# The first x block in five transfers instead of two, and its casts in a new order

## The chip, the cores and the metric

The kernel runs on one core of one Trainium2 chip. The metric is the device time of one execution in microseconds (us); less is better. Times given as "span" are those of one profiled execution, from its first to its last instruction.

## The reference

Two layers follow each other. The first is a causal convolution with weights of its own at every position: `weight_gen` (8 x 4096 x 8 heads x 7 taps) goes through a softmax over the 7 taps, and each position of `x` (8 x 4096 x 192) becomes, head by head (24 columns each), the weighted sum of itself and the six positions before it. The second is a feed-forward layer with squared ReLU.

```python
w = weight_gen - np.max(weight_gen, axis=-1, keepdims=True)
w = np.exp(w)
w = w / (np.sum(w, axis=-1, keepdims=True) + 1e-09)
x_pad = np.concatenate([np.zeros((B, pad, D)), x], axis=1)      # pad = 6
x_unf = x_pad[:, idx, :].reshape(B, S, K, H, group)             # seven shifted views
x = np.einsum('bshk,bskhg->bshg', w, x_unf).reshape(B * S, D)   # 32768 x 192
h = np.maximum(x @ w_in, 0.0)                                   # 192 x 2048
out = h * h @ w_out                                             # 2048 x 192
```

## The kernel before

All matmuls are in fp16 with f32 sums. The 32768 positions are cut into sub-blocks of 512. The first two blocks hold one sub-block each, all later blocks two. Within a sub-block the convolution works on five tiles of 128 rows of x, each 104 rows after the one before (`NT = 5`, `STEP = 104`); a tile covers 104 outputs (the last 96) and the rows ahead that their taps need.

For each tile three things must exist before TensorE can convolve it: the softmax weights of its 128 rows (`wr`), a banded matrix made of them on VectorE (`bd`, `st_band`, L406), and the x tile in fp16 (`xt`). The convolution's matmuls (L466 in the first two blocks) write `yp` in PSUM; two casts make it `y` (ScalarE L476, VectorE L477). `y` goes through w_in (L566, later L581) to `h`, ScalarE applies ReLU (L595), VectorE squares (L599), and TensorE multiplies by w_out (L630).

The order of all work is written out by hand: engines run their instructions in program order, and the transfers of one queue are issued in program order too. Two queues matter here, that of SyncE (SP in the profile) and that of GpSimd (POOL). A transfer of f32 data that POOL issues may cast to fp16 on the way; SP's transfers do not cast, so what SP loads is cast by an engine afterwards.

The start, which is where the change lies, goes as follows.

- SP issues the loads of the first 1024 positions' weights (`s0.load`, three transfers, `wg`, L219), then the first sub-block's x in f32 (`x_load_f32(0)`, `x_st`): tile 0 alone (L317) and tiles 1 to 4 in one transfer (L327), both through `block_load`. Then the first half of w_in in f32 (`load_w_in(w_st, 0, nc.sync)`, three transfers, L133 and L135).
- POOL waits at a small copy (`gate`, L716) until the softmax's reciprocals exist, and then issues the second sub-block's x, the second half of w_in and the next weights. A second such copy (L746) waits for `w_st`; behind it POOL issues w_out (L183) and more.
- TensorE spins on zeros (L697) until the softmax of the first rows is scaled (`v_first`, L266). It then brings the rows of weights to the partitions where the tiles want them by matmuls with a selection matrix (`select_rows`, L383, eight matmuls a tile), first the five tiles of sub-block 0, then the five of sub-block 1, and then convolves.
- ScalarE takes the exponentials (L244), casts x tile 0 (`x_cast`, L342), copies the selected rows of tiles 0 and 1 out of PSUM (`copy_rows`, L391), casts x tiles 1 and 2 in one instruction, copies the rows of tiles 2 to 4, casts x tiles 3 and 4, copies the rows of sub-block 1 in one instruction, casts one part of `w_st` to `w_i` (`cast_w_in`, L740), and casts `y`. VectorE makes the five bands, casts the other half of `y`, and then the other part of `w_st` (L740 as well).

In the code before, the part of this order that the change touches reads:

```python
x_cast(0, nc.scalar.copy, 0, 1)
o0, o1, ring = (ps_o, "o0"), (ps_o, "o1"), (ps_h, "h")
select_rows(0, s0, ROW_ORDER, (o1, ring, ring, ring, o0))
copy_rows(0, ROW_ORDER[:2])
x_cast(0, nc.scalar.copy, 1, 3)
copy_rows(0, ROW_ORDER[2:])
x_cast(0, nc.scalar.copy, 3, NT)
```

After the start, blocks follow each other with the w_in units of one block, the w_out matmuls of the block before and the convolution of the block after woven into each other by written plans.

Of the kernel before, what the change touches and what calls it, by code (L numbers as in the profile page):

```python
# [9 lines left out]
def kernel(  # L10
# [26 lines left out]
    nc = tc.nc  # L37
# [3 lines left out]
    B, S, D = x.shape  # L41
# [9 lines left out]
    P = 128  # L51
    TB = 512
    NBB = S // TB
# [12 lines left out]
    NT = 5  # L66
# [4 lines left out]
    ROW_ORDER = (0, 1, 2, 3, 4)  # L71
# [57 lines left out]
    x_st = {}  # L129
# [167 lines left out]
    def rows(ap2d, t0, width):  # L297

        return bass.AP(
            tensor=ap2d.tensor, offset=ap2d.offset + t0 * width,  # L300
            ap=[[width, P], [STEP * width, NT], [1, width]],
        )

    def ends(b):
        rs = PARTS.get(b, (R,))
        return [P * sum(rs[: i + 1]) for i in range(len(rs))]

    def tile_start(j, i):

        t1 = (j % NBB + 1) * TB  # L310
        return TB - P if i == NT - 1 and t1 in ends(j // NBB) else starts[i]

    def block_load(j, dst, src, width, eng):
        t0 = (j % NBB) * TB
        first, last = int(t0 == 0), NT
        if first:
            eng.dma_start(out=dst[:, 0], in_=src[0:P, :])  # L317
        a = t0 + tile_start(j, NT - 1)
        if a != t0 + starts[-1]:
            last = NT - 1  # L320
            eng.dma_start(out=dst[:, last], in_=src[a : a + P, :])
        ap = rows(src, t0 + starts[first], width)
        ap = bass.AP(
            tensor=ap.tensor, offset=ap.offset,
            ap=[ap.ap[0], [STEP * width, last - first], ap.ap[2]],
        )
        eng.dma_start(out=dst[:, first:last], in_=ap)  # L327
# [4 lines left out]

    def x_load_f32(j):
        x_st[j] = p_one.tile([P, (R + HALO) * HK], f32, name="x_st", tag="ex")
        block_load(
            j, x_st[j][:, 0 : NT * D].rearrange("p (t d) -> p t d", t=NT), x[j // NBB], D, nc.sync
        )

    def x_cast(j, copy, lo, hi):
        if j not in x_t:  # L340
            x_t[j] = p_x.tile([P, NT, D], f16, name="xt")
        copy(  # L342
            out=x_t[j][:, lo:hi].rearrange("p t d -> p (t d)"),
            in_=x_st[j][:, lo * D : hi * D],
        )
# [23 lines left out]
    def select_rows(j, s, tiles, places):  # L369

        if j not in wr_t:
            wr_t[j] = p_wr.tile([P, NT, HP, SL * 2], f16, name="wr")
        n = len(tiles) // len(places)
        for m, i in enumerate(tiles):
            if m % n == 0:
                pool, tag = places[m // n]
                prs = pool.tile([P, n, H * SL], f32, name="pr", tag=tag)
                pr_t[(j, i)] = prs
            pr = prs[:, m % n]
            a = max(j % NBB * TB + tile_start(j, i), 0) - s.t0  # L380
            for r in range(s.r):
                c = a + FIRST - 1 - r
                nc.tensor.matmul(  # L383
                    out=pr, lhsT=sel[:, c : c + P],
                    rhs=s.v[:, HALO + r].rearrange("p g c e -> p (g c e)"),
                    start=(r == 0), stop=(r == s.r - 1),
                )

    def copy_rows(j, tiles, n=1):
        for i in tiles[::n]:  # L390
            nc.scalar.copy(  # L391
                out=wr_t[j][:, i : i + n].rearrange("p t g c -> p t (g c)"),
                in_=pr_t.pop((j, i)),
            )
# [271 lines left out]
    with nc.allow_low_precision("fp16 matmul pipeline"), tc.manual_schedule():  # L666
# [39 lines left out]
        s0.load(nc.sync, s0_cuts)  # L706
        w_st = p_wg.tile([P, (R + HALO) * HK], f32, name="w_st", tag="wg")[:, 0 : NQ + NQ // 2]
        x_load_f32(0)
        row_select()
        load_w_in(w_st, 0, nc.sync)  # L710
# [10 lines left out]
        x_cast(0, nc.scalar.copy, 0, 1)  # L721
        o0, o1, ring = (ps_o, "o0"), (ps_o, "o1"), (ps_h, "h")
        select_rows(0, s0, ROW_ORDER, (o1, ring, ring, ring, o0))
        copy_rows(0, ROW_ORDER[:2])
        x_cast(0, nc.scalar.copy, 1, 3)
        copy_rows(0, ROW_ORDER[2:])
        x_cast(0, nc.scalar.copy, 3, NT)
        for i in ROW_ORDER:
            st_band(0, (i,))
        select_rows(1, s0, ROW_ORDER, (o1,))  # L730
# [76 lines left out]
        for j in range(len(plans), NBLK - 1):  # L807
            a = BLOCKS[j + 1][0]
# [102 lines left out]
        j = NBLK - 1  # L911
# [44 lines left out]
```

## Time and profile before

| What | Value |
|---|---|
| Time of the timed runs | 730.38 us, median of 3 (729.42 to 730.4) |
| Span of the profiled execution | 728.4 us, 1.98 us under that median |
| TensorE busy | 722.0 us, 99% of the span |
| VectorE, ScalarE, GpSimd busy | 625.8 us (86%), 612.0 us (84%), 98.5 us (14%) |
| First w_in matmul of block 0 | at 12.20 us |
| Granted TensorE clock | 1.000 |

The profile is one execution; its own time is the span, and what the timed runs have beyond it lies around the first and last instruction or in differences from execution to execution. Lines of the profile name an engine, the line of the kernel (L342 is line 342), what is written and read, and how long. "PE" is TensorE, "DVE" VectorE, "ACT" ScalarE, "SPq" the instructions of SyncE that issue transfers. An idle time in brackets ends with what released it. A busy TensorE includes times that are modelled, so 99% says that it always had something to do and not that it ran at its peak.

### The profile page before, as it was taken

The numbers are of one execution on the slowest core, as the hardware profiler recorded it, in microseconds if no ns is written. First come the engines' busy times: TensorE is split into PE (matmuls) and PEld (weight loads), VectorE is DVE, ScalarE is ACT, GpSimd is POOL, SyncE is SP. The second block draws the span as 40 slices with busy tenths as digits, with TensorE's granted clock in tenths as the row PEclk, the third lists the DMA queues.
The fourth block names the chain that finished last, engine by engine and source line by source line (L and its number), as shares of the span: only waits on it lengthen the run. The fifth ranks groups of instructions, "written<-read, shape, count | busy, mean of one in ns | idle before, by whom it ended". The sixth has DMA issues, their size and how long they took to land.

```text
span 728.4 us, 31046 instructions
## 1 busy us (share of the span) xinstructions
PE 722.0 (99%) x14078; PEld 530.1 (73%) x14078; DVE 625.8 (86%) x839; ACT 612.0 (84%) x731; POOL 98.5 (14%) x146
## 2 busy tenths in 40 slices
PE   8999999999999999999999999999999999999998
PEld 5668877777777777777777777777777777777777
DVE  7999997998898998888988888988888988778753
ACT  6998888888888888888888888888888888888883
POOL 7231223411001100011001010010000110001000
PEclk9999999999999999999999999999999999999999
DMA  9664465676245443356432554343544325444112
GB/s 193 128 113 106 82 125 89 128 142 138 78 71 133 99 84 68 75 116 125 83 62 58 135 104 88 66 74 110 114 78 87 57 53 117 67 87 77 30 46 67
DMA packets 126272, 68.30 MB, mean 94 GB/s; under 512 B 85353, under 2 KB 122556, under 8 KB 125628
## 3 DMA queue, kind: packets, MB, share of 16 engines
q0 software_dynamic: 46192, 19.43, 22.9%
q1 hardware_dynamic: 79804, 46.79, 22.5%
q8 instruction: 110, 1.80, 1.1%
q14 instruction: 22, 0.18, 0.1%
q10 hardware_dynamic: 144, 0.10, 0.0%
HBM read 50.18 MB, written 28.70 MB: 108 GB/s over the span
## 4 chain that ended last, share of the span: by engine, by line
PE 98%; DMA 1%; SPq 0%; ACT 0%; issue 0%; ACTq 0%
PE o L630 47%; PE h L581 44%; PE yp L502 4%; PE h L566 2%; PE yp L536 1%; DMA w_st<-in_moe_w_in_dram 1%; SPq L219 0%; PE yp L466 0%; ACT w_i L740 0%; SPq L135 0%; SPq L133 0%; ACT y L476 0%; SPq L327 0%; SPq L317 0%; ACT o_sb L644 0%
## 5 line engine op out<-in xcount | busy, mean ns | idle before, releaser
L595 ACT ACTIVATE t<-h 128x1024 f16<-128x1024 f32 x512 | 496.6, 1027 | 60.1 <-PE h L581 58.4
L630 PEld LDWEIGHTS <-g 64*128 64x128 f16 (+1 forms) x8032 | 344.3, 94 | 55.2 <-issue 2.3
L630 PE MATMUL o<-w_o,g 64*128 64x192 f16 (+1 forms) x8032 | 380.1, 243 | 0.1
L599 DVE TENSOR_TENSOR g<-t 128x2048 f16<-128x2048 f16 (+1 forms) x287 | 307.4, 1105 | 28.7 <-ACT t L595 28.3
L581 PE MATMUL h<-y,w_p 64*128 64x512 f16 x2400 | 291.7, 376 | 0.0
L581 PEld LDWEIGHTS <-w_p 64*128 64x128 f16 x2400 | 113.9, 94 | 94.8
L406 DVE TENSOR_TENSOR bd<-wr,mask 128x4160 f16<-128x4160 f16 (+4 forms) x90 | 149.5, 1685 | 1.2 <-ACT wr L391 1.2
L646 DVE TENSOR_TENSOR o_sb<-o,o_sb 128x384 f32<-128x384 f32 x123 | 68.4, 556 | 61.4 <-ACT o_sb L644 60.3
L327 POOL DMA_DIRECT2D xt<-in_x_dram x63 | 52.6, 838 | 415.4 <-PE yp L502 362.5
L644 ACT COPY o_sb<-o 128x384 f32<-128x384 f32 x129 | 61.6, 477 | 45.7 <-PE o L630 44.4
L581 PE MATMUL h<-y,w_i 64*128 64x512 f16 x576 | 70.5, 376 | 0.0
L581 PEld LDWEIGHTS <-w_i 64*128 64x128 f16 x576 | 30.5, 94 | 21.7 <-issue 1.2
L502 PEld LDWEIGHTS <-xt 128*32 128x32 f16 x2000 | 24.6, 95 | 10.6 <-issue 10.6
L266 DVE TENSOR_TENSOR v_big<-ex,rcp 128x112 f16<-128x112 f32 (+5 forms) x180 | 29.9, 237 | 2.1 <-DMA vd<-v_big 1.1
L512 DVE CAST y<-yp 128x1024 f16<-128x1024 f32 x25 | 30.4, 1218 | 0.0
L502 PE MATMUL yp<-bd,xt 128*32 128x104 f16 (+1 forms) x2000 | 28.4, 210 | 0.0
L244 ACT ACTIVATE ex<-wg 128x560 f32<-128x560 f32 (+5 forms) x40 | 26.3, 659 | 1.2 <-DMA wg<-in_weight_gen_dram 1.2
L251 DVE TENSOR_REDUCE ssum<-ex 128x80 f32<-128x560 f32 (+5 forms) x40 | 25.6, 639 | 1.3 <-ACT ex L244 1.3
L512 ACT CAST y<-yp 128x1024 f16<-128x1024 f32 x25 | 25.2, 1007 | 0.0
L258 DVE RECIPROCAL rcp<-ssum 128x64 f32<-128x64 f32 (+4 forms) x39 | 23.0, 589 | 1.4
L317 POOL DMA_DIRECT2D xt<-in_x_dram x7 | 3.9, 555 | 120.4 <-PE yp L502 109.4
L361 POOL DMA_DIRECT2D wr<-v_first x24 | 13.0, 559 | 24.0 <-DVE v_first L266 23.8
(42 smaller groups left out, 111.9 us busy)
## 6 DMA issues: line engine op xcount, KB each, us to landing
out_dram<-o_sb SPq DMA_DIRECT2D x63, 384.0 KB
xt<-in_x_dram POOLq DMA_DIRECT2D x42, 240.0 KB, 4.9
wg<-in_weight_gen_dram SPq DMA_DIRECT2D x4, 1064.0 KB
xt<-in_x_dram POOLq DMA_DIRECT2D x21, 192.0 KB, 5.0
wr<-vd SPq DMA_DIRECT2D x38, 80.0 KB
vd<-v_big SPq DMA_DIRECT2D x5, 512.0 KB
y<-y SPq DMA_DIRECT2D x100, 24.0 KB
wg<-in_weight_gen_dram SPq DMA_DIRECT2D x3, 616.0 KB
```

The source lines that it names most:

```text
L244: nc.scalar.activation(out=self.ex[:, lo:hi].rearrange("p r g k e -> p (r g) k e"), in_=self.wg[:, lo:hi].rearrange("p r (g e) k -> p (r g ...
L266: eng.tensor_tensor(out=bass.AP(tensor=v.tensor, offset=v.offset + lo * H * SL + lo % SL * 2 + g * SL * 2, ap=[list(v.ap[0]), [H * SL + 2, ...
L327: eng.dma_start(out=dst[:, first:last], in_=ap)
L406: nc.vector.tensor_tensor(out=bd_t[j][:, H * lo : H * (lo + len(tiles) * n)].rearrange("p (g m c) -> p g m c", g=shape[1], c=2 * SL), in0= ...
L502: nc.tensor.matmul(out=yp[p0 : p0 + 32, k - k0, a:b], lhsT=x_t[s][:, i, c0 : c0 + 32], rhs=bd[:, head // 2, e, 0 : b - a], start=True, sto ...
L512: copy(out=y[:, k0 : k0 + 2], in_=yp)
L581: nc.tensor.matmul(out=h[:, half], lhsT=w_in_chunk(w, u, slot, half), rhs=y_t[j][r0 : r0 + RT, k], start=(slot == 0), stop=(slot == NK - 1 ...
L595: nc.scalar.activation(out=t1[:, e], in_=h, func=ActF.Relu)
L599: nc.vector.tensor_tensor(out=g[:, a : e + 1], in0=t1[:, a : e + 1], in1=t1[:, a : e + 1], op=AluOp.mult)
L630: nc.tensor.matmul(out=oo[:, cc * Dm : (cc + 1) * Dm], lhsT=g[r0 : r0 + n, cc * P : (cc + 1) * P], rhs=w_o[r0 : r0 + n, fc, :], start=(fc ...
L644: nc.scalar.copy(out=o_sb, in_=o[0][:, c])
L646: nc.vector.tensor_tensor(out=o_sb, in0=o[1][:, c], in1=o_sb, op=AluOp.add)
```

## The change

The first sub-block's x is loaded in five transfers, one for each tile of 128 rows, all issued by SP one after the other at the place where the two stood. Each tile is cast by an instruction of its own. The casts of tiles 1 and 2 stand ahead of the row copies, the five row copies follow without a break, and the casts of tiles 3 and 4 come after them. What is loaded, cast and copied is the same; no other line differs.

```diff
     def x_load_f32(j):
         x_st[j] = p_one.tile([P, (R + HALO) * HK], f32, name="x_st", tag="ex")
-        block_load(
-            j, x_st[j][:, 0 : NT * D].rearrange("p (t d) -> p t d", t=NT), x[j // NBB], D, nc.sync
-        )
+        for i in range(NT):
+            a = max(j % NBB * TB + tile_start(j, i), 0)
+            nc.sync.dma_start(
+                out=x_st[j][:, i * D : (i + 1) * D], in_=x[j // NBB, a : a + P, :]
+            )
...
         select_rows(0, s0, ROW_ORDER, (o1, ring, ring, ring, o0))
-        copy_rows(0, ROW_ORDER[:2])
-        x_cast(0, nc.scalar.copy, 1, 3)
-        copy_rows(0, ROW_ORDER[2:])
-        x_cast(0, nc.scalar.copy, 3, NT)
+        x_cast(0, nc.scalar.copy, 1, 2)
+        x_cast(0, nc.scalar.copy, 2, 3)
+        copy_rows(0, ROW_ORDER)
+        x_cast(0, nc.scalar.copy, 3, 4)
+        x_cast(0, nc.scalar.copy, 4, NT)
         for i in ROW_ORDER:
             st_band(0, (i,))
```

## The prediction

> **What bounds the kernel now.** First the page: TensorE holds the span, and the chain that ended last is TensorE's but for a little DMA.
>
> ```profile
> PE 722.0 (99%) x14078; PEld 530.1 (73%) x14078; DVE 625.8 (86%) x839; ACT 612.0 (84%) x731; POOL 98.5 (14%) x146
> ...
> PE 98%; DMA 1%; SPq 0%; ACT 0%; issue 0%; ACTq 0%
> ```
>
> The change lies in the first 12 us, so the chain of waits in order of time says what that part costs (start us, us, what):
>
> ```profile
> 2.67 0.43 SPq L327
> ...
> 3.15 0.51 SPq L133
> ...
> 3.70 0.59 SPq L135
> ...
> 4.33 6.39 DMA w_st<-in_moe_w_in_dram
> ...
> 10.83 0.83 ACT w_i L740
> 11.66 0.49 ACT y L476
> ...
> 12.20 3.17 PE h L566 x16
> ```
>
> From 12.20 us on the chain is TensorE without a gap worth naming (the table of busy time by stage gives it 17.00 of 17.00 us from 13 to 30). So the change is worth what it does to the 12.20, one for one, and to nothing else. What sets 12.20 is not x: it is w_st, the first half of w_in, cast at 10.83, and then y, cast behind it on the same in-order ScalarE.
>
> ScalarE in order of time shows what x costs (start, busy, then in brackets the idle time before and who ended it):
>
> ```profile
> 4.57 0.34 ACT L342 CAST xt<-x_st 128x192 f16<-128x192 f32 x1
> 7.58 0.45 ACT L391 CAST wr<-pr 128x64 f16<-128x64 f32 x2 [2.68 <-PE pr L383]
> 8.81 0.51 ACT L342 CAST xt<-x_st 128x384 f16<-128x384 f32 x1 [0.78 <-DMA x_st<-in_x_dram]
> 9.23 0.43 ACT L391 CAST wr<-pr 128x64 f16<-128x64 f32 x3
> 9.54 0.53 ACT L342 CAST xt<-x_st 128x384 f16<-128x384 f32 x1
> 9.95 0.45 ACT L391 CAST wr<-pr 128x320 f16<-128x320 f32 x1
> 10.83 0.83 ACT L740 CAST w_i<-w_st 128x768 f16<-128x768 f32 x1 [0.43 <-DMA w_st<-in_moe_w_in_dram]
> ```
>
> The cast at 8.81 waits 0.78 us for the four-tile x transfer, and row copies 2 to 4 wait behind it. That reaches the bands on VectorE and the first convolution:
>
> ```profile
> 7.90 1.09 DVE L406 TENSOR_TENSOR bd<-wr,mask 128x832 f16<-128x832 f16 x2 [0.75 <-ACT wr L391]
> 9.47 1.60 DVE L406 TENSOR_TENSOR bd<-wr,mask 128x832 f16<-128x832 f16 x3 [0.47 <-ACT wr L391]
> 11.54 0.69 DVE L477 CAST y<-yp 128x512 f16<-128x512 f32 x1 [0.47 <-PE yp L466]
> ```
>
> Two paths thus end nearly together: the convolution at 11.54, w_st's cast at 11.66.
>
> Why the four tiles take 6.14 us (2.67 to 8.81) is in the trace's packet records: on most DMA engines their 768-byte packets run from 4.1 to 6.0, but one packet begun at 5.66 took 1854 ns. That engine moved its last 13 x packets from 7.51 to 7.91 and only then its share of w_st, to 10.23; the others were through with w_st by 8.95. In the DMA view for 8.95 to 10.3 the queue of SP has 17 packets left:
>
> ```profile
> q1 hardware_dynamic: 17, 0.03, 5.7%
> ```
>
> **The change part by part.**
>
> *The convolution path.* The three row copies no longer sit behind a cast that waits. The selections give a tile every 0.25 us (78 matmuls in 2.44 us, eight a tile), so the last copy ends near 8.8. The bands, 0.545 us each (1.09 for two), then run without the 0.47 us gap from 7.90 to 10.63 instead of to 11.07: 0.44 us won, and the convolution ends near 11.10. The casts of tiles 1 and 2 (0.34 each) fit in ScalarE's idle 2.68 us ahead of 7.58; those of tiles 3 and 4 (0.68) come after 8.8, and the next copy must wait anyway for the second tile's selections (done at 9.65). ScalarE's casts grow from 1.38 to 1.70 us, hidden by those two idle stretches; without them 0.32.
>
> *When the tiles land.* The trace has no x transfer alone but tile 0. The loads of this size or near it on SP were usable 2.08, 2.32 and 2.43 us after issue (wg at 0.81, 1.26, 1.72, used at 2.89, 3.58, 4.15), tile 0 within 2.37. With issues at 2.67, 3.14, 3.61 and 4.08 this gives 5.1, 5.6, 6.0 and 6.5. The far end is the four-tile row, 6.14 after issue: tile 2 at 9.28. I take the near end for tiles 1 and 2, as they are the same shape as tile 0, and count the far end as a rival.
>
> The Trainium skill, "DMA: Bandwidth & Descriptors", "Rules for kernel authors", speaks against the change: many small transfers are to be joined into a large one, and its section on the anatomy of one DMA gives about 2.0 us of fixed cost each. Paid one after the other, three more would be an estimate of 6 us. The three wg loads, usable 0.57 to 0.69 us apart, say that these costs overlap.
>
> *Three more issues on SP.* One costs 0.47 us (0.43 and 0.04 to the next), three 1.41. All three w_st issues are moved behind them: from 3.15, 3.70, 4.29 to 4.56, 5.11, 5.70. The next item on SP, a row move (L361), started at 7.18 on VectorE's release, so SP has the room (6.3 against 7.18). POOL's issues keep their place; its gate at L746 waits for w_st as well (10.18), and behind it stand the four w_out loads. In the built order SP's transfers take eight completion semaphores in turn, and with five x transfers they wrap earlier: each w_st issue now waits for one of the wg loads. These were used at 2.89, 3.58 and 4.15, the issues' turns are 4.56, 5.11, 5.70: nothing, by 1.5 us or more. Later SP transfers still wait for the one eight before them, as now.
>
> *What of the 1.41 reaches w_st's landing.* Its packets now begin at 5.56, 2.4 us after issue, since x is ahead of them in each engine; a transfer that finds its queue empty begins 1.33 to 1.40 after issue (x tile 0: 2.20 to 3.53). So moved to 4.56 they begin near 5.96, 0.4 later. The rest is 8 packets of 159 ns and 8 of 84 ns an engine, 1.94 us: done at 7.9, used (0.6 later, as with the last packet at 10.23 and the cast at 10.83) at 8.5. ScalarE gets to that cast at 10.3 at the earliest, so the 1.41 is covered by 1.8 us of slack on an undisturbed engine. On an engine that stops on x as before, w_st queues behind it and lands when it does now, cost nothing. If the cover is gone, 0.4 to 1.41.
>
> *The sum.* With the stop as now: w_st cast 10.83, y 11.66, TensorE 12.20, change 0. Without a stop: ScalarE free at 10.3, w_st's cast to 11.13, y (convolution at 11.10) to 11.62, TensorE at 11.65, 0.55 us won. This 0.55 is the floor, since select, copies and bands do not move. I take a little over nothing, -0.1 us. The profiled span is 728.4 us, the median of the timed runs 730.38, so 1.98 us lie around it or differ between executions; I leave them as they are: 728.4 - 0.1 + 1.98 = 730.3.
>
> **The rivals.**
>
> *Hidden anyway (the forecast, 0.64).* x's wait is taken away and w_st holds the end. 0 to -0.55 us from the profiled span, with as much scatter of runs as they have shown (729.42 to 730.4): 729.6 to 730.8.
>
> *w_st becomes later (slower, 0.28).* The stop of 1.85 us belongs to an engine and a moment and not to x; falling on w_st's packets, which now end 0.4 us later among POOL's (the packets of 2048 bytes went from 84 to about 140 ns beside them), it lands after 10.72. It decides from the point where the last w_st packet ends after 10.23. Price: at most the whole 1.41, 0.45 for eight slow packets, and up to 0.45 if the issues that now carry a wait cost 0.15 more each (an estimate from L361's 0.59 to 0.63 against 0.43): 2.3, middle 1.6, so 732.0. Against it: the 1.8 us slack. Since w_out follows the same gate, that wait moves along.
>
> *Tile 2 late (slower, in the 0.28 too).* All five copies now stand behind the casts of tiles 1 and 2, two of them did not before. It decides from a landing after 7.24. At the far end, 9.28: copies from 9.62, bands to 12.5, convolution 12.97, y 13.5, +1.3 us.
>
> *The stop was the form's (faster, 0.08).* If reading four rows of a partition 104 rows apart made the 1854 ns packet, five contiguous reads lose it; 0.55 us by the profile. More than that needs timed executions which wait longer than the profiled one; the 1.98 us leave room for it, nothing shows it.
>
> **How the numbers follow.** 0.2% is 1.46 us, about what a measurement of this kernel can tell from no change. The forecast lies within. Of the slower cases' 0.28, 0.25 is given to above 1.46, since both have prices up to 1.3 or 2.3 and the trace shows only one execution's stops. The faster case counts in full, 0.08, with 0.02 for timed executions that differ from the profiled one in other ways: 0.10. Same: 0.65. The range runs from 729.3 (the floor, less 0.5 for scatter) to 732.0, the middle of the w_st case.
>
> **What would show it.** Right: five issues of 0.43 us on SP, w_st from 4.56; two casts before 7.58; five copies on end without a DMA wait; bands ending near 10.6; w_st's cast at 10.8 or before, first h matmul between 11.6 and 12.2. Wrong: a DMA wait on the cast of tile 1 or 2 past 7.24; the cast of w_st released by DMA after 11; TensorE idle after 13 us, at the w_out matmuls above all.

## The result and the profile after

The changed kernel is slower. Its median over 16 timed runs is 731.22 us (730.15 to 735.12), that of the kernel before, in 16 runs on the same chip, 730.04 us (728.97 to 731.46). The ratio of the times is 1.0025, with an interval of 1.0014 to 1.0035: about 1.8 us. The 0.2% (1.46 us) that the prediction took as the smallest loss to be told from no change lies inside the interval, so it is clear that the kernel is slower, and not that it is slower by more than that. The medians differ by only 1.18 us because the added time is not the same in every run. Of the 16, 11 had a granted clock of 0.999 or more over the whole span, and their spans have a median of 729.3 us. The other 5 show 0.995 to 0.998, and their spans have a median of 731.5 us. The kernel before was run 103 more times beside the experiments below; its spans have a median of 728.2 us, and no run was under 0.999. So the change costs 1.1 us where the clock holds and 3.3 us where it does not: (11 x 1.1 + 5 x 3.3) / 16 is 1.8 us.

The profiled execution (733.96 us, span 732.3 us) is one of those five. Busy time by engine and the chain that ended last, from its page:

```profile
PE 724.1 (99%) x14078; PEld 531.2 (73%) x14078; DVE 625.9 (85%) x839; ACT 613.0 (84%) x733; POOL 98.3 (13%) x146
...
PE 91%; DVE 3%; DMA 2%; ACT 1%; issue 1%; SPq 1%; POOL 0%; DVEq 0%; ACTq 0%
```

The chain of waits in order of time (start us, us, what), which in the kernel before reached the first w_in matmul at 12.20:

```profile
4.10 0.43 SPq L337
...
4.58 0.43 SPq L133
...
5.05 0.59 SPq L135
...
5.68 5.75 DMA w_st<-in_moe_w_in_dram
...
11.54 0.83 ACT w_i L743
12.37 0.49 ACT y L478
...
12.90 4.73 PE h L568 x16
```

It is still w_st that ends last, and everything on its path is later: the first issue by 1.43 us (4.58 for 3.15), the cast by 0.71, the first w_in matmul by 0.70. The 16 matmuls after it took 3.17 us before and take 4.73 now. ScalarE in order of time (start, busy, then in brackets the idle time before and who ended it) shows that x itself behaves as planned:

```profile
5.65 0.61 ACT L344 CAST xt<-x_st 128x192 f16<-128x192 f32 x2 [0.45 <-DMA x_st<-in_x_dram]
7.71 1.15 ACT L393 CAST wr<-pr 128x64 f16<-128x64 f32 x5 [1.45 <-PE pr L385]
8.76 0.61 ACT L344 CAST xt<-x_st 128x192 f16<-128x192 f32 x2
9.81 0.42 ACT L393 CAST wr<-pr 128x320 f16<-128x320 f32 x1 [0.45 <-PE pr L385]
11.54 0.83 ACT L743 CAST w_i<-w_st 128x768 f16<-128x768 f32 x1 [1.30 <-DMA w_st<-in_moe_w_in_dram]
```

Two casts lie ahead of the copies, the five copies run on end, and the only long wait is for w_st: 1.30 us on an idle ScalarE. On VectorE the bands have lost their gap and the convolution's result is read earlier (11.11 against 11.54):

```profile
8.03 2.60 DVE L408 TENSOR_TENSOR bd<-wr,mask 128x832 f16<-128x832 f16 x5 [0.75 <-ACT wr L393]
11.11 0.69 DVE L479 CAST y<-yp 128x512 f16<-128x512 f32 x1 [0.48 <-PE yp L468]
```

In the DMA view for 8.95 to 10.3, where SP's queue had 17 packets left before, it has 78:

```profile
q1 hardware_dynamic: 78, 0.13, 34.6%
```

TensorE is therefore done with the convolution at 11.05 and idle for 1.86 us. Of this wait the table of busy time by stretches shows the second half of the damage. Its columns are the stretch, its length, then busy us and instructions of PE, PEld, DVE, ACT and POOL, the granted clock, the DMA share and GB/s. Kernel after:

```profile
9.46:12.87 3.41, 1.56 (x91) 1.30 (x88) 2.93 (x6) 1.74 (x3) 2.24 (x5) 1.00 1.18 184
12.87:16.28 3.41, 3.38 (x10) 0.66 (x9) 1.94 (x2) 1.42 (x2) 1.82 (x3) 0.50 1.29 230
```

In the first stretch TensorE was busy for 1.56 of 3.41 us (46%); in the next one, exactly as long, its granted clock is half, and 10 matmuls fill it. Half of 3.41 is 1.7 us lost (an estimate). The profiled execution's 3.9 us over the span before are thus 0.7 (later start), 1.7 (clock) and about 1.2 of waits in the middle: between 60 and 240 us TensorE was busy 178.71 us, against 179.90 before. The page has those in the w_out group, where the kernel before has 0.1:

```profile
L632 PE MATMUL o<-w_o,g 64*128 64x192 f16 (+1 forms) x8032 | 380.5, 243 | 1.3 <-DVE o_sb L648 1.3
```

These 1.2 us are this execution's own, as the next section shows; 0.3 of the 3.9 us are not assigned.

### The profile page after: what moved, and what is told of

It is laid out like the page before. It is cut to its first block, busy times and chain, and to the rows that moved or that the text cites. A ratio compares the mean times of both kernels' runs of the same rounds, so it can differ in the third digit from the quotient of the medians.

```text
span 732.3 us, 31051 instructions
## 1 busy us (share of the span) xinstructions
PE 724.1 (99%) x14078; PEld 531.2 (73%) x14078; DVE 625.9 (85%) x839; ACT 613.0 (84%) x733; POOL 98.3 (13%) x146
## 4 chain that ended last, share of the span: by engine, by line
PE 91%; DVE 3%; DMA 2%; ACT 1%; issue 1%; SPq 1%; POOL 0%; DVEq 0%; ACTq 0%
PE o L632 44%; PE h L583 41%; PE yp L504 4%; PE h L568 2%; DVE g L601 1%; DMA vd<-v_big 1%; PE yp L538 1%; DVE bd L408 1%; DMA w_st<-in_moe_w_in_dram 1%; ACT t L597 1%; DMA wr<-v_first 1%; SPq L337 0%; DVE o_sb L648 0%; DVE v_big L266 0%; DVE v_first L266 0%
## 5 line engine op out<-in xcount | busy, mean ns | idle before, releaser
L568 PE MATMUL h<-y,w_i 128*128 128x512 f16 (+1 forms) x64 | 14.8, 417 | 1.9 <-ACT y L478 1.9
```

The source lines that it names most:

```text
L568: nc.tensor.matmul(out=out, lhsT=lhsT, rhs=rhs, start=(n == 0), stop=(n == 1), skip_group_check=True, tile_position=(r0, 0),)
```

## The experiments

The theory after the result: x's five transfers delay w_st's three issues on SP, w_st then ends the wait later than anything else, and TensorE's longer pause sometimes costs the clock as well. Rivals: the form of x's transfers (more, smaller, with more completions) or the new order on ScalarE is what costs; and, for the clock, that it is a mere accident of the runs. Three steps follow: which part of the change it is, what the clock has to do with it, and why w_st lands as late as it does.

A table of all runs comes first. "Low clock" counts runs at 0.998 or less; "span" is the median of the others, against 728.1 to 728.3 of the kernel before; "w_st cast" and "first h" are the starts of w_st's cast on ScalarE and of the first w_in matmul in the profiled execution.

| Kernel | Ratio to before | Low clock | Span | w_st cast | First h |
|---|---|---|---|---|---|
| before | 1 | 0 of 103 | 728.2 | 10.83 | 12.20 |
| after | 1.0025 (1.0014 to 1.0035) | 5 of 16 | 729.3 | 11.54 | 12.90 |
| e1_five_old_order | 1.0017 (1.0009 to 1.0026) | 2 of 12 | 729.3 | 11.79 | 13.16 |
| e2_two_copies_first | 0.9999 (0.9991 to 1.0008) | 0 of 12 | 727.85 | 10.06 | 11.61 |
| e12_copies_first_again | 1.0001 (0.9992 to 1.0010) | 0 of 11 | 728.3 | 10.67 | 12.04 |
| e4_before_late_w | 1.0033 (1.0020 to 1.0046) | 5 of 8 | 729.3 | 11.98 | 13.35 |
| e5_w_after_one | 1.0008 (1.0000 to 1.0017) | 1 of 11 | 728.85 | 10.92 | 12.29 |
| e8_w_after_three | 1.0011 (1.0002 to 1.0019) | 1 of 11 | 728.9 | 10.79 | 12.16 |
| e9_two_w_between | 1.0022 (1.0013 to 1.0031) | 4 of 11 | 729.4 | 12.07 | 13.44 |
| e10_before_one_pad | 0.9997 (0.9988 to 1.0006) | 0 of 11 | 727.7 | 10.05 | 11.61 |
| e11_before_two_pads | 1.0019 (1.0011 to 1.0028) | 3 of 11 | 729.0 | 11.44 | 12.81 |
| e13_three | 0.9999 (0.9990 to 1.0008) | 0 of 11 | 728.0 | 10.02 | 11.58 |
| e3_after_spin | 1.0038 (1.0022 to 1.0055) | 3 of 9 | 730.0 | 11.59 | 12.95 |
| e7_after_wide_spin | 1.0022 (1.0012 to 1.0032) | 0 of 9 | 729.7 | 11.84 | 13.21 |
| e14_after_pool_later | 1.0083 (1.0068 to 1.0099) | 4 of 4 | none | 11.18 | 12.54 |
| e15_big_pads | 1.0043 (1.0031 to 1.0055) | 4 of 5 | 730.0 | 12.65 | 14.02 |
| e16_touch_w | 1.0038 (1.0025 to 1.0051) | 3 of 6 | 729.8 | 11.94 | 13.31 |

In the profiled executions that kept their clock, the span less the start of the first h is 715.9 to 716.8 us, whatever the kernel: 716.2 for the kernel before (728.4 - 12.20), 716.1 for e1, e10 and e13, 716.4 for e7. So the first h moves the end one for one, and the rest of the span is the same to within 0.9 us. In e4, e11 and e15, whose profiled executions lost the clock for one window, it is 717.8, 718.1 and 718.3, that is 1.6 to 2.1 more. After has 719.4; so the 1.2 us in its middle do not belong to the lost clock as such. (e3 and e14 lost it too, but have further pauses.)

**Which part costs: the transfers, the order, or w_st's place.** e1 takes the five transfers alone, with the order of before on ScalarE. Against the changed kernel its edit is:

```diff
-        x_cast(0, nc.scalar.copy, 1, 2)
-        x_cast(0, nc.scalar.copy, 2, 3)
-        copy_rows(0, ROW_ORDER)
-        x_cast(0, nc.scalar.copy, 3, 4)
-        x_cast(0, nc.scalar.copy, 4, NT)
+        copy_rows(0, ROW_ORDER[:2])
+        x_cast(0, nc.scalar.copy, 1, 3)
+        copy_rows(0, ROW_ORDER[2:])
+        x_cast(0, nc.scalar.copy, 3, NT)
```

> The five transfers alone: the row copies and casts of ScalarE stand in the order of before (copies of tiles 0 and 1, cast of tiles 1 and 2, copies of tiles 2 to 4, cast of tiles 3 and 4). Theory (three more issues ahead of w_st make w_st late, and the longer pause of TensorE ahead of the first h matmul costs the clock in part of the executions): w_st's issue at 4.58 and its cast near 11 to 11.5 as in the changed kernel, so the executions at clock 1.000 are 0.4 to 0.9 us slower than before; the convolution ends near 11.1 because each tile's transfer has landed in time, so some executions lose the clock for one window and are 2 to 3 us slower. Median 0.8 to 1.5 us above before. Rival (the new order of ScalarE's copies and casts is what costs): same as before within 0.3 us and a clock of 1.000 in all executions.

e2 does the other half, five copies ahead of the casts with the two transfers of before; e12 is the same kernel again in a later group of runs.

```diff
-        copy_rows(0, ROW_ORDER[:2])
+        copy_rows(0, ROW_ORDER)
         x_cast(0, nc.scalar.copy, 1, 3)
-        copy_rows(0, ROW_ORDER[2:])
         x_cast(0, nc.scalar.copy, 3, NT)
```

> Two transfers as before, and all five row copies ahead of the casts of tiles 1 to 4: the order alone, no issue added. Theory (w_st's issue is what moves the end): w_st is issued at 3.15 as before and its cast is at 10.8 or earlier, TensorE's first h matmul at 11.7 to 12.2, median -0.5 to 0 us from before; the pause of TensorE ahead of it is at most 1.1 us, so the clock stays at 1.000 in nearly all executions. Rival (the earlier end of the convolution alone is enough to lose the clock): 3 or more of 16 executions show a clock below 0.9995 and lie 2 us or more above the others.

> The kernel with two x transfers and all row copies ahead of the casts of tiles 1 to 4, timed again for a closer ratio. Theory (its bulk at spans of 727.5 to 728.0 is the floor that the selections, copies and bands set, and before reaches it in about a third of its executions): 0.2 to 0.4 us below before in the median, with a few executions 1.5 us above. Rival (no difference): ratio 1.000 with an interval of less than 0.1% to each side.

e4 keeps x's two transfers and its order, and only pushes w_st back on SP, by three loads of 32 bytes a partition that nobody uses:

```diff
         x_load_f32(0)
+        pad = const.tile([P, 3, 8], f32, name="pad")
+        for i in range(3):
+            nc.sync.dma_start(out=pad[:, i], in_=x[0, 0:P, 8 * i : 8 * i + 8])
         row_select()
         load_w_in(w_st, 0, nc.sync)
```

> The kernel before with three small transfers (32 bytes a partition, not read) on SP between x and w_st: w_st is issued 1.41 us later as in the changed kernel, while x keeps its two transfers and ScalarE its order. Theory (the issue's delay reaches w_st's landing): w_st's cast 0.3 to 1.4 us later, executions at clock 1.000 0.4 to 0.9 us above before, and some lose the clock since TensorE's pause grows (from 0.7 us to 1.1 or more, less than in the changed kernel, whose convolution also ends earlier). Rival (what costs is the five transfers' landing or their many packets, not the delay): within 0.3 us of before.

The order alone is worth nothing that can be measured, twice. The transfers alone cost 0.17%, and w_st's later place, behind three added loads of 4 KB each, costs 0.33% with x as before. The two intervals, and that of the change, overlap. ScalarE in the profiled e4:

```profile
9.55 0.42 ACT L391 CAST wr<-pr 128x320 f16<-128x320 f32 x1 [0.49 <-PE pr L383]
11.98 0.83 ACT L743 CAST w_i<-w_st 128x768 f16<-128x768 f32 x1 [2.00 <-DMA w_st<-in_moe_w_in_dram]
```

ScalarE stands idle for 2.00 us until w_st is there. That the form of x's transfers costs is thereby not needed to explain the loss. If it is w_st's place, five transfers with w_st further ahead should be rid of the loss. Against the changed kernel, e5 issues w_st behind the first x tile and casts x after the copies (shown, without the body of `x_load_f32`), e8 issues it behind the third (`range(3)` and `range(3, NT)`) and keeps the order of the change on ScalarE:

```diff
-        x_load_f32(0)
+        x_load_f32(0, range(1))
         row_select()
         load_w_in(w_st, 0, nc.sync)
+        x_load_f32(0, range(1, NT))
...
-        x_cast(0, nc.scalar.copy, 1, 2)
-        x_cast(0, nc.scalar.copy, 2, 3)
         copy_rows(0, ROW_ORDER)
-        x_cast(0, nc.scalar.copy, 3, 4)
-        x_cast(0, nc.scalar.copy, 4, NT)
+        for i in range(1, NT):
+            x_cast(0, nc.scalar.copy, i, i + 1)
```

> Five x transfers as in the changed kernel, but SP issues w_st directly behind x tile 0 and tiles 1 to 4 behind w_st; ScalarE makes all five row copies first and then casts tiles 1 to 4 one by one. The number of transfers is that of the changed kernel, only w_st's place in the queue differs. Theory (w_st's place in SP's queue is the cause): w_st issued at 2.67, its cast at 10.4 or earlier, first h matmul at 11.6 to 12.3, no execution with a clock of 0.998 or below, median within 0.4 us of before. Rival (five transfers are the cause wherever they stand: more issues, more semaphores, slower reads): 0.8 us or more above before.

> Five x transfers, w_st issued behind tile 2 (0.47 us later than in the kernel before, by one issue), tiles 3 and 4 behind it; ScalarE's order as in the changed kernel. Theory (w_st's place in the queue): between before and the changed kernel, w_st's cast at 10.4 to 11.2, 0 to 0.6 us above before, at most 1 execution at a clock of 0.998 or below. If tiles 3 and 4 land behind w_st's packets later than 9.8, the convolution gets late instead and adds up to 0.5 us. Rival (five transfers are the cause): as the changed kernel, 0.8 us or more above before.

e9 does it with the two transfers of before: tile 0, then w_st, then tiles 1 to 4 in one, and the order of e2 (`True` loads tile 0, `False` the rest; only the calls are shown).

```diff
-        x_load_f32(0)
+        x_load_f32(0, True)
         row_select()
         load_w_in(w_st, 0, nc.sync)
+        x_load_f32(0, False)
```

> Two x transfers as before, with w_st issued between them (0.47 us earlier than before), and all five row copies ahead of the casts of tiles 1 to 4. Theory (w_st's landing is what ends last wherever it is late): w_st's cast follows the row copy of the second sub-block without a wait at about 10.1, first h matmul at 11.6, so the slower ones of the executions of before (spans of 728.8 to 730.2) become rarer: median 0 to 0.5 us below before. Rival (x in its last place now ends late: four tiles behind w_st): casts of tiles 1 to 4 wait past 9.7, the convolution ends after 11.5, 0 to 1 us above before.

ScalarE in e5:

```profile
9.56 1.14 ACT L345 CAST xt<-x_st 128x192 f16<-128x192 f32 x4 [0.78 <-DMA x_st<-in_x_dram]
10.60 0.42 ACT L394 CAST wr<-pr 128x320 f16<-128x320 f32 x1
10.92 0.83 ACT L743 CAST w_i<-w_st 128x768 f16<-128x768 f32 x1
```

in e8:

```profile
9.96 0.60 ACT L345 CAST xt<-x_st 128x192 f16<-128x192 f32 x2 [0.81 <-DMA x_st<-in_x_dram]
```

and in e9:

```profile
10.93 0.93 ACT L351 CAST xt<-x_st 128x384 f16<-128x384 f32 x2 [1.79 <-DMA x_st<-in_x_dram]
```

In e5 and e8 w_st's cast no longer waits for DMA, and by the ratios more than half of the loss is gone (0.08% and 0.11% left of 0.25%), though each still has one run of 11 at a low clock, which the theory of e5 had excluded. What is left has changed hands: the last x tiles are now late (0.78 us in e5, 0.81 in e8). In e9 the load that goes last is late by more, 1.79 us, and the loss is whole again: its theory (0 to 0.5 us below before) missed, and its rival, x late in the last place, named what happened, at a higher price than it gave (1.7 us for 0 to 1). In these three kernels, what stands last in SP's queue is what is waited for.

How far may w_st be pushed back? e10 and e11 are e4 with one and with two of the small loads (`range(1)`, `range(2)`), and e13 is a version of the change that adds one transfer only: tile 0, tiles 1 and 2, tiles 3 and 4, with w_st behind all three.

```diff
-        block_load(...)
+        nc.sync.dma_start(out=x_st[j][:, 0:D], in_=src[0:P, :])
+        for i in (1, 3):
+            nc.sync.dma_start(out=x_st[j][:, i * D : (i + 2) * D]..., in_=...)
...
-        copy_rows(0, ROW_ORDER[:2])
         x_cast(0, nc.scalar.copy, 1, 3)
-        copy_rows(0, ROW_ORDER[2:])
+        copy_rows(0, ROW_ORDER)
         x_cast(0, nc.scalar.copy, 3, NT)
```

> The kernel before with one small transfer (not read) on SP between x and w_st: w_st issued 0.47 us later, near 3.6. Theory 1 (a transfer whose descriptors stand ready in the engines' queues behind x reads without long stops, one that starts as soon as it is issued does not): at 3.6 w_st is still ready, near 5.0, ahead of the end of x's packets at 5.6, so its packets stay as before, no more than 2 of the 128 packets of 4096 bytes above 600 ns, and the time is within 0.3 us of before, clock 1.000. Theory 2 (every later issue reaches the landing in proportion): a third of what three such transfers cost at full clock, 0.4 to 0.6 us above before, some executions at 0.998.

> The same with two small transfers: w_st issued 0.94 us later, near 4.1, ready near 5.5, when x's packets end. Theory 1 (queueing behind x): the edge, part of the long packets come back, 0.3 to 1.2 us above before. Theory 2 (in proportion): 0.8 to 1.0 us above before, one in four executions at a clock of 0.998 or below.

> Three x transfers (tile 0, tiles 1 and 2, tiles 3 and 4) ahead of w_st, the cast of tiles 1 and 2 ahead of the five row copies, that of tiles 3 and 4 behind: the same aim as the change with one added issue in place of three. Theory 1 (queueing behind x): w_st keeps its packets, first h matmul at 11.7 to 12.2, within 0.3 us of before and a clock of 1.000. Theory 2 (in proportion): 0.3 to 0.6 us above before.

ScalarE in e10:

```profile
10.05 0.84 ACT L743 CAST w_i<-w_st 128x768 f16<-128x768 f32 x1
```

and in e11:

```profile
11.44 0.83 ACT L743 CAST w_i<-w_st 128x768 f16<-128x768 f32 x1 [1.15 <-DMA w_st<-in_moe_w_in_dram]
```

One added issue (0.47 us) costs nothing: w_st is there before ScalarE comes to it. Two cost 0.19%, three 0.33%. So the first issue fits into slack that the second (0.94 us) exceeds; whether each one after that has its own price, the intervals do not decide. e13 is within the noise of the kernel before, and so is e2: no version tried beats it. The start of e2, e10 and e13 at 11.58 to 11.61 is the floor that the prediction gave (11.65), but the kernel before is usually nearer to it than its profiled 12.20 says. The median span of its timed executions, 728.2, less 716.2 gives 12.0, so about 0.4 us is left to win (an estimate).

**The clock.** If TensorE's pause costs the clock, filling it with matmuls on zeros should keep it. e3 adds 12 matmuls of 156 columns behind the first convolution, e7 adds 6 of 512 columns (the results are not used). The edit of e7, against the changed kernel; e3 differs in the number and width:

```diff
         st_conv_first(0)
+        wp = ps_o.tile([P, TB], f32, name="wp2", tag="o0")
+        for i in range(6):
+            nc.tensor.matmul(out=wp, lhsT=warm[:, 0:P], rhs=warm, start=True, stop=True)
         cast_w_in(1, nc.vector.tensor_copy)
```

> The changed kernel with 12 matmuls on zeros (128x156, their result is not read) between the first convolution and the first h matmul, to fill TensorE's pause. Theory (part of the loss is the clock, halved for one window of 3.4 us after a window in which TensorE was busy 46%): no execution with a clock of 0.998 or below, the slow tail (731 to 733 us of span) goes, median 0.4 to 0.9 us above before, which is what the late w_st leaves. Rival (all of the loss is the late w_st, and the clock varies with something else): the spread and the median stay as in the changed kernel, 1.2 to 1.8 us above before, with clocks of 0.995 to 0.998 in about 6 of 16 executions.

> The changed kernel with 6 matmuls on zeros of 512 columns (result not read) between the first convolution and the first h matmul: about 1.3 us of TensorE work in 12 instructions, where the 12 narrow ones were 0.98 us in 24. Theory (the clock is lost when TensorE is busy less than about half of a window of 3.4 us): the window around the pause goes from 46% to over 70% busy, no or at most 1 of 10 executions at a clock of 0.998 or below, median 0.5 to 1.1 us above before and no tail. Rival (the pause can't be filled: added instructions run into the instruction fetch, as the gap of 1.53 us after the fifth h matmul of the narrow spin may show, and that loses the clock as well): a gap of 1 us or more among the first h matmuls, and 2 or more executions at 0.998 or below.

TensorE in e3 (the bracket "issue" is time in which the engine waited for nothing that the profile shows):

```profile
10.69 0.98 PE L749 MATMUL wp<-warm 128*128 128x156 f16 x12
12.95 1.13 PE L568 MATMUL h<-y,w_i 128*128 128x512 f16 x5 [1.28 <-ACT y L478]
15.61 1.77 PE L568 MATMUL h<-y,w_i 64*128 64x512 f16 x4 [1.53 <-issue]
```

and in e7:

```profile
10.96 1.47 PE L749 MATMUL wp<-warm 128*128 128x512 f16 x6
13.21 2.10 PE L568 MATMUL h<-y,w_i 128*128 128x512 f16 x10 [0.77 <-ACT y L478]
```

e3 was a miss, with the low clocks that its rival expected: 0.98 us of work left 1.28 us of pause, and a second pause of 1.53 us came up behind the fifth h matmul, where the engine waited for nothing that the trace names; in the profiled execution the clock was lost behind it, and it was low in 3 of 9 runs. e7 leaves 0.77 us of pause, and no run of 9 lost the clock. It stays 0.22% slower, since w_st is as late as before (its full-clock span is 1.4 us over that of the kernel before). With 5 of 16 in after, none of 9 is no proof by itself. All kernels together say more. In those whose profiled first w_in matmul began by 12.29 (before, e2, e5, e8, e10, e12, e13), 2 of 170 runs had a low clock; in those where it began at 12.81 or later and nothing filled the pause (after, e1, e4, e9, e11, e15, e16), 26 of 69 had. (e3 and e7 fill the pause, and e14 delays other loads too.) So a low clock is no accident of the runs: it comes with the late start, and late w_st and lost clock are two costs with one cause. The busy time in the 3.41-us window just ahead shows how far TensorE's pause explains it:

| Execution | TensorE busy in a window of 3.41 us | Next window |
|---|---|---|
| e15 | 1.36 (40%) | half clock |
| e4, e3 | 1.40 and 1.41 (41%) | half clock |
| e14 (a later pause, from 18.4) | 1.47 (43%) | half clock |
| after | 1.56 (46%) | half clock |
| e16 | 1.56 (46%) | full |
| e11 | 1.68 (49%) | half clock |
| e9, e8 | 2.00 (59%) and 2.04 (60%) | full |
| e1, two windows in a row | 2.30 and 2.12 (67%, 62%) | full |
| e5 | 2.24 (65%) | full |
| before | 2.65 (78%) | full |

In each of the six the clock is half for one window of 3.41 us and then full again. In the traces that kept the clock no such window after the start is under 59% busy, but for one: e16 kept it behind a window as little busy as that of after.

```profile
11.46:14.87 3.41, 1.56 (x9) 0.57 (x10) 2.96 (x4) 1.93 (x3) 3.24 (x5) 1.00 1.22 252
14.87:18.29 3.42, 3.42 (x95) 1.53 (x93) 1.60 (x3) 3.42 (x5) 3.42 (x3) 1.00 1.48 178
```

So six of seven windows under half busy were followed by half clock and none with 59% or more, but the busy time alone does not decide it. What else counts stays open: in e16 the 1.56 us are nine w_in matmuls at the end of the window, in after 91 small matmuls at its start, and in e15 eight w_in matmuls (1.36 us) were not enough. e1 shows how a pause can stay without effect. Its pause, 2.37 us, is longer than after's 1.86, but by the edges in its own clock record it fell into two windows:

```profile
8.45:11.87 3.42, 2.30 (x117) 1.96 (x113) 2.67 (x6) 1.12 (x5) 1.56 (x5) 1.00 1.24 199
11.87:15.28 3.41, 2.12 (x12) 0.70 (x14) 2.90 (x3) 2.40 (x4) 3.37 (x5) 1.00 1.17 227
```

The edges lie elsewhere in each execution, which fits that only some lose the clock. The Trainium skill, "TensorE: Matmul & The Clock Gate", in its part on the clock gate, describes such a free-running window of about 3.4 us and says that one idle window brings the clock to half; under "HAM oscillation — how this bites in real kernels" it puts the rule as no TensorE gaps above about 3.4 us. The window and its half clock agree with these traces, the rule does not: in the six windows that lost it the longest single pause was 1.4 to 3.0 us.

**Why w_st lands so late.** In the packet records, w_st's packets begin only a little later than before, as predicted, but end later by more. Each row is one execution, and e2 and e12, the same kernel, show how far two executions differ:

| Execution | First and last w_st packet (us) | Packets of 4096 bytes over 600 ns, of 128 |
|---|---|---|
| before | 5.56 to 10.24 | 0 |
| e2 | 5.56 to 9.38 | 1 |
| e12 (e2 again) | 5.54 to 10.07 | 1 |
| e10 (one issue more) | 5.40 to 9.33 | 1 |
| e13 (one issue more) | 5.44 to 9.02 | 6 |
| e11 (two) | 5.72 to 10.78 | 6 |
| after (three) | 5.69 to 10.94 | 7 |
| e4 (three) | 6.11 to 10.89 | 7 |
| e1 (three) | 5.74 to 11.22 | 9 |
| e5 (w_st behind one x tile) | 3.94 to 8.52 | 7 |
| e8 (w_st behind three x tiles) | 4.83 to 9.02 | 10 |

Three theories were tried. First, the traffic that POOL issues runs into w_st: e14 holds it back until w_st is there, which delays other loads and makes the kernel slower by itself, so that only the landing is read.

```diff
-        nc.gpsimd.tensor_copy(out=gate, in_=s0.rcp[:, FIRST, 0, 0:1])
+        nc.gpsimd.tensor_copy(out=gate, in_=w_st[:, 0:1])
         x_load(1)
```

> The changed kernel, with the first of POOL's two gates waiting for w_st instead of for the softmax's reciprocals: none of POOL's loads runs beside w_st's. Only w_st's landing is read here; the total grows, as the second sub-block's x and the second half of w_in come later. Theory POOL (POOL's transfers and their descriptors, issued from 6.28 on, slow w_st's reads): few packets of 4096 bytes above 600 ns, w_st's last packet at 9.5 or earlier, its cast by 10.2. Theory start (w_st's own reads are long where the queue ahead of it is empty): the long packets stay, at 5.7 to 8, last packet only 0.3 to 0.8 us earlier (its tail had POOL's packets among it), cast at 10.7 to 11.3.

Second, SP's queue runs empty ahead of w_st, and what follows pays for it: e15 is e4 with three full loads (128x192) in place of the small ones, which keep the queue filled. Third, the first reads of w_in are slow: e16 is e4 with the three small loads taken from w_in's rows. The edits of e15 and e16 follow, both against the kernel before.

```diff
+        pad = const.tile([P, 3, D], f32, name="pad")
+        for i in range(3):
+            nc.sync.dma_start(out=pad[:, i], in_=x[0, 128 * i : 128 * i + P, :])
```

> As the kernel with three small transfers ahead of w_st, but each of them a tile of 128 x 192 in f32 (not read), so x and they keep the engines busy to about 6.4 and w_st, ready near 6.0, queues behind them. 295 KB more are moved ahead of w_st. Theory queue (a transfer that waits behind others reads without long stops): no more than 3 packets of 4096 bytes above 600 ns, w_st's last packet at 10.0 to 10.6, no later than with the small ones (10.89) in spite of the added bytes, and a median 1 to 3 us above before, below that of the small ones (732.85). Theory bytes and issue only: last packet 0.8 us later than with the small ones, about 11.7, median 733 or more.

```diff
+        pad = const.tile([P, 3, 8], f32, name="pad")
+        for i in range(3):
+            c = 512 * i
+            nc.sync.dma_start(out=pad[:, i], in_=moe_w_in[0:P, c : c + 8])
```

> As the kernel with three small transfers ahead of w_st, but they read 32 bytes of each of w_in's first 128 rows (at columns 0, 512 and 1024; not read) in place of x: w_st's first 128 rows have been read from once before w_st starts. Theory first touch (the long packets are the first reads of w_in's rows, wherever w_st stands): no more than 3 packets of 4096 bytes above 600 ns, last packet by 10.2, cast by 10.8, median 0 to 0.6 us above before. Theory queue: as with the small transfers from x, 5 or more long packets, last packet near 10.9, cast near 11.5 to 12, median 1.5 to 3 us above before.

None is borne out. With POOL's loads away (e14) the last packet ends at 10.61 instead of 10.94, and 9 packets are long; 0.33 us is within what e2 and e12 differ by. That fits the second theory, but e15 does not: w_st ends later still, at 11.93, with 4 long packets, as in the rival of bytes and issue only (about 11.7, median 733 or more; it was 733.07). e16 touches 32 bytes at two places of each 4096-byte row ahead of w_st; w_st ends at 11.19 with 6 long packets, as the rival had it, though a first touch of all the bytes was not tried. The long packets do not settle it either: e13, e5 and e8 have 6 to 10 of them and land by 9.02. So it stays open why w_st ends so late.

What single executions show is that w_st's 768 KB take 3.6 us (e13) to 5.5 us (e1) from first to last packet. With all of x ahead, the last packet came at 9.02 to 10.24 behind no or one added issue (five kernels) and at 10.61 to 11.93 behind two or more (nine). The first packet differs by only 0.3 us in the mean of the two groups (5.50 and 5.82, e15 with its added bytes left out).

## Why the prediction was wrong

The forecast was no change (730.3, with 0.65 on "same"); it came out slower, which had 0.25. The time lies in the range (731.22 within 729.3 to 732.0). Point by point, by its steps:

- *The convolution path* was right. Bands from 8.03 to 10.63 (said: 7.90 to 10.63), the convolution done at 11.05, 0.42 us earlier than before, the casts hidden.
- *When the tiles land* was right: tiles 1 and 2 were cast from 5.65 on with 0.45 us of wait, 0.5 us later than the 5.1 said for tile 1 and still long before the copies. "Tile 2 late" did not occur.
- *Three more issues on SP* was right in size: w_st's first issue at 4.58, for 4.56 said. The waits that the prediction gave to the w_st issues cost nothing: the issues took 0.43, 0.59 and 0.58 us, where the first took 0.51 before.
- *What of the 1.41 reaches w_st's landing* failed. The start of the packets was foreseen nearly (5.96 said, 5.69 found: 1.11 us after the issue, not 1.40; the first load of all in the kernel before, with nothing ahead of it, already shows 1.03, issued at 0.81 and begun at 1.84). The end was not. The step took the pace of an undisturbed engine, 1.94 us, and so got 7.9 and "1.8 us of slack", though the trace of before itself showed 4.68 us from the first packet to the last (5.56 to 10.24). The load is there when the slowest of its engines is done, and that was at 10.94. Its second thought, that an engine which stops would hold w_st where it is now, made x the owner of the stop. In after, x's packets are all done by 6.15 with none over 600 ns, and w_st's own have the long ones, up to 1345 ns; e4 and e16 have the same late end with x unchanged. Of the 1.41 us, 0.71 reached the cast in the profiled execution; by the median full-clock spans it was 1.1 at TensorE (729.3 - 728.2). Why w_st's packets take so long there stays open.
- *A term that was missing*: TensorE's clock. Both changes lengthen its pause, the convolution that ends earlier on the one side and w_st on the other, from 0.72 to 1.86 us. The executions that lose it, 5 of 16, are 2.2 us longer by the two groups' spans, which is 0.7 us in the mean of the 16. Without this term the change would stand at about 0.15%, under the 0.2% that the prediction took as no change; e7, where the clock holds, has 0.22% with 0.3 us of that its own later start.
- *The sum* rested on one profiled execution in which the kernel before started at 12.20; its timed ones start near 12.0, so that a cast of w_st "as late as now" would already have cost them 0.2 us. Of the 1.98 us that it puts around the span, 1.65 to 1.84 lie there in every run with both numbers; the rest is scatter.
- The rival "w_st becomes later" named the mechanism and the signs: the cast of w_st released by DMA after 11 (it came at 11.54), and a price from 0.4 us up, with 1.6 us in the middle; 1.8 us was measured, of which only 1.1 are the rival's. Its reason, the stop falling on w_st's packets, fits the long ones of after, but e13, e5 and e8 have as many and land early. That the median lies inside the range is partly luck: 0.7 of the 1.8 us come from the clock, which the range did not contain.
- The Trainium skill's rule of joining small transfers ("DMA: Bandwidth & Descriptors", "Rules for kernel authors") pointed to the right side. Its price, the estimate of 6 us, is far from the 1.8 us found; the section on the anatomy of one DMA, which gives that fixed cost, is about transfers that GpSimd issues, and SP issued these. It was not x's transfers that paid, but the load behind them.

## What to carry to other kernels

Before splitting a load, look at what stands behind it in the same queue, and ask when that one is needed: each added issue pushes it back by the time of an issue (0.47 us here), and slack has to be read from the last packet of the slowest engine, not from a mean pace. There may be room for one more issue and not for two, so try the smallest split first. Where a change shortens the work ahead of a wait of TensorE, add up its busy time in windows of 3.4 us: where it is under half, the clock is at stake for a window afterwards (in six of the seven such windows here), in some executions only, so that one profile need not show it.

## What the runs showed of the hardware that was not expected

- Six windows of 3.41 us in which TensorE was busy for 40 to 49%, with no single pause over 3.0 us, were followed by exactly one such window at half clock, an estimated 1.7 us lost; one with 46% (e16) and all with 59% or more were not.
- Of w_st's 128 packets of 4096 bytes, 0 took over 600 ns in the kernel before and 7 after, up to 1345 ns, where the mean of before is 187 ns. How late w_st is issued does not set their number: e5 issues it earlier than before and has 7, e10 later and has 1. Taking POOL's traffic away (e14: 9) or touching a few bytes of the rows first (e16: 6) did not remove them.
- Twelve added matmuls brought up a pause of 1.53 us elsewhere on TensorE (e3), behind the fifth h matmul, which waited for no other engine; six wider ones did not (e7). Its cause is open.
